# A front end in another order: the first tile in halves, power operands on VectorE, scales in pairs, an early exp table

## The chip, the cores and the metric

The kernel runs on one core of one Trainium2 chip. A core has five engines that run side by side, each through its own list of instructions in order: TensorE (PE in the profile) multiplies matrices, VectorE (DVE), ScalarE (ACT) and GpSimd (POOL) do the rest, and SyncE (SP) issues the transfers (DMAs). Engines wait for each other by semaphores. Where work stands in an engine's list is decided when the kernel is built. The metric is the device time of one execution in microseconds (us), as the median of several.

## The reference

The input x has 2048 tokens of 512 columns in fp32. A first LayerNorm feeds two branches, and these are multiplied:

```python
xn = layernorm(x)                                # no learned scale or bias, eps 1e-5
# A: local attention, 32 heads of 16, window of 8 tokens with dilation 2
q, k, v = split(xn @ wqkv)                       # 512 -> 3 x 512
logits = q . k[pos - 2*w] * 16**-0.5             # w = 0..7; -1e9 ahead of the first token
s = softmax(logits) . v[pos - 2*w] @ wo          # 512 -> 512
# B: an MLP over the columns
h = gelu_tanh(layernorm(xn) @ w1 + b1)           # 512 -> 1376
g = silu(h @ w2 + b2)                            # 1376 -> 512
out = x + s * g
```

## The kernel before, in words

**Tiles.** The even tokens and the odd tokens are kept apart (parity c = 0 and 1), since a window with dilation 2 stays within one parity. Each parity is 8 tiles of 128 tokens, one token to a partition. The 32 heads are 4 blocks of 8 heads. A unit u = 0..7 is one parity with one block of heads. The MLP runs over 4 chunks of 512 tokens and 11 blocks of hidden columns.

**Numbers.** Nearly all matmuls run in fp16 with operands split into a high and a low half, and three products (high by high, low by high, high by low) are added up. Each weight is first scaled by a power of two from its own sum of squares: a Square on ACT with an accumulator, a small matmul on TensorE that adds over partitions (`total`, L400 for two columns), and a chain of one-column operations on DVE (L411, `half_exp` L418, `up` L424, `down` L429). Then come the high half (ACT) and the low half (DVE, L494 for wqkv).

**The front.** For parity 0, `ln0` (L550) takes the tiles group by group, as GROUPS lists them; LOADS says in which order the DMAs bring tiles of x and the first block of wqkv. For each tile, DVE makes statistics (`stats`, L535) and aggregates them to mean and variance (L536). `factors` (L503) then makes, on POOL, for a whole group: an operand from the variance (L514); its power -1/2, which is the scale for both LayerNorms at once (L517); for groups that are normalized on ACT, a bias (L521); another operand (L524) and its power (L526); and two products (L528, L530), which give the scale that attention needs (cT). With this, DVE normalizes a tile (L571), or ACT does, with scale and bias, where the first tile of the group is in ACT_Y (`y_act`, L539). TensorE transposes it by four matmuls with an identity (L578). For tiles 2 and 3 (FP), ACT copies the transposed tile in fp32 (L584), and the first projections of these two tiles run in fp32 on the unscaled weights as they land (L651); all other tiles are cut into halves at once (L590 on ACT, L592 on DVE). In front of the first transpose, 30 idle matmuls (L1063, WAKE0 + WAKE) stand in TensorE's list; the last four wait for the first normalized tile. Parity 1 goes through `ln1` (L598), later and beside the attention of parity 0.

**Units.** `qkv` (L623) first makes a scale cs for its unit: by POOL group by group for unit 0 (L629), by one small ACT operation for the others (L627). For each tile follow 12 fp16 matmuls (L644) into PSUM and an ACT operation that scales them into the buffer U of the unit (L661). There are two such buffers, used in turn, and the matmuls of a unit's first tile wait in the plan for all earlier users of q, k and v of that U. DMAs then bring the rows that a token's window needs from neighbouring partitions (L670, L675, L676). `attention` (L689) has, on DVE, four products of 2048 columns (L704) with four sums (L707), the maximum (L727), the subtraction (L728); then exp on ACT (L730); and on DVE the sum (L732), the reciprocal, the quotient, four products with v (L760) and sums (L755), two of which POOL does in part (L783, L784). The result is transposed by a DMA into oT.

**MLP and end.** `mlp1` (L899) has 12 matmuls for a block of hidden columns (L914), gelu on ACT (L931), the high half on ACT (L935), and the low half on DVE (L939) or by TensorE and ACT. `mlp2` (L953) has 12 matmuls (L961) into four accumulators z and, after the last block of a chunk, silu on ACT (L977, in the last chunk L972), whose results go to HBM for three chunks. ACT holds one function table at a time, and exp, gelu and silu each need their own. `wo_first` (L830) and `wo_last` multiply the attention by wo, then by silu's results, and add x (`finish`, L821 on DVE, L823 on POOL) and store (L824). The last tile is finished in two halves (L880 to L889).

**The plan.** None of this runs in the order of the code. `Plan` (L93) collects every operation with an engine, a planned duration, what it reads and writes, a priority, and sometimes a slack, which makes it look ready later than it is. It then plays the operations through against each other, by the planned durations, and picks at each step the ready operation that can start first, by priority among those close together; buffers of a ring (`Ring`) are given out in this order too. The order that results is written to each engine. A change of a duration, a priority or a dependency can so move operations anywhere in the kernel. The main loop at the end of the code gives each unit a number of MLP steps (`mlp([7, 7, 6, 4, 7, 7, 2, 0][u])`), which fill TensorE between the projections.

## Time and profile before

The times of three runs are 421.53, 421.61 and 422.89 us; the median is 421.61.

| | before |
|---|---|
| profiled execution, its own time | 421.77 us |
| span of the profiled execution | 420.0 us |
| granted TensorE clock, mean | 1.00 |
| PE busy | 410.1 us (98%), 2107 matmuls |
| PE weight loads | 209.5 us (50%), beside the matmuls |
| DVE busy | 387.7 us (92%) |
| ACT busy | 211.6 us (50%) |
| POOL busy | 91.8 us (22%) |
| chain that ended last | PE 78%, DVE 10%, POOL 3%, issue 3%, DMA 2%, ACT 1% |
| moved by DMA | 44.83 MB, 107 GB/s on average |

The span is what lies between the first and the last instruction of the profiled execution; its own time is 1.77 us longer. The chain that ended last is found by going back from the last instruction, each time to what released it. The costliest groups are the matmuls of L914 (115.5 us), L644 (114.5) and L961 (111.4), then DVE's products and sums at L704 (73.1), L707 (72.8) and L760 (63.5), and gelu at L931 (31.4). In rows of the profile, `f` is a tile of 512 columns, `lw` and `mx` are small ones, `prod` one of 2048, `ps`, `mh` and `z` are PSUM accumulators, and an entry such as `[0.35 <-ACT f L977]` behind a row gives the idle time of the engine ahead of it and what ended it.

### The profile page before, as it was taken

To read this page: it belongs to the slowest core of one execution; us is meant where nothing else is said; L and a number is where in the kernel's file an instruction comes from. 1 tells how busy PE (TensorE), PEld (TensorE's weight loads), DVE (VectorE), ACT (ScalarE), POOL (GpSimd) and SP (SyncE) were. 2 spreads that over 40 slices of the span, in tenths; PEclk is the share of its full clock that TensorE was granted. 3 is DMA by queue.
4 is the path that set the end of the run, shared out by engine and by line. 5 is a ranking of instruction groups with operands and counts; after the bars stand their busy time and mean duration, and the time that the engine had idled before them with its cause. 6 is when DMAs were issued, how large, how long until landed. Compare 5 with 4: busy or idle time off the path is not lost.

```text
span 420.0 us, 5549 instructions
## 1 busy us (share of the span) xinstructions
PE 410.1 (98%) x2107; PEld 209.5 (50%) x2107; DVE 387.7 (92%) x365; ACT 211.6 (50%) x314; POOL 91.8 (22%) x166
## 2 busy tenths in 40 slices
PE   7989999999999999999999999999999999999995
PEld 5556544445554465445544654454445544444442
DVE  4867999999999999899999999999999989999983
ACT  3899983953437842853358335334121393236400
POOL 7810200000463043002500430052002500250031
PEclk9999999999999999999999999999999999999999
DMA  8964440120025247611262022006423383007152
GB/s 298 413 234 140 126 163 0 61 91 0 2 87 126 77 108 163 154 39 26 87 151 100 2 87 52 1 20 193 150 85 123 88 209 111 2 0 204 52 144 102
DMA packets 42666, 44.83 MB, mean 107 GB/s; under 512 B 27496, under 2 KB 27936, under 8 KB 42128
## 3 DMA queue, kind: packets, MB, share of 16 engines
q1 hardware_dynamic: 42640, 44.49, 35.0%
q8 instruction: 16, 0.26, 0.3%
q14 instruction: 10, 0.08, 0.1%
HBM read 23.53 MB, written 7.34 MB: 74 GB/s over the span
## 4 chain that ended last, share of the span: by engine, by line
PE 78%; DVE 10%; POOL 3%; issue 3%; DMA 2%; ACT 1%; SPq 0%; DVEq 0%; POOLq 0%; ACTq 0%
PE ps L644 22%; PE z L961 22%; PE mh L914 21%; PE ps L830 6%; PE z L830 2%; DVE prod L704 2%; PE mh L644 2%; DVE prod L760 2%; DVE L L707 2%; PE mh L830 1%; PE ps L914 1%; DMA U<-U 1%; DVE f L614 1%; POOL lw L517 1%; DMA f<-in_A_x_dram 1%
## 5 line engine op out<-in xcount | busy, mean ns | idle before, releaser
L914 PE MATMUL mh<-yT,w 128*128 128x512 f16 (+1 forms) x504 | 115.5, 379 | 0.1
L644 PE MATMUL ps<-wq,yT 128*128 128x384 f16 x684 | 114.5, 326 | 0.9 <-ACT U L661 0.8
L961 PE MATMUL z<-w,h 128*128 128x512 f16 x480 | 111.4, 379 | 0.6 <-ACT f L977 0.6
L644 PEld LDWEIGHTS <-yT 128*128 128x128 f16 x744 | 72.7, 98 | 49.5 <-issue 1.1
L914 PEld LDWEIGHTS <-w 128*128 128x128 f16 (+1 forms) x528 | 52.8, 100 | 61.3 <-issue 0.4
L961 PEld LDWEIGHTS <-h 128*128 128x128 f16 x480 | 47.0, 98 | 56.0 <-issue 1.1
L704 DVE TENSOR_TENSOR prod<-U 128x2048 f32<-128x2048 f32 x32 | 73.1, 2290 | 1.6 <-DMA U<-U 0.6
L707 DVE TENSOR_REDUCE L<-prod 128x128 f32<-128x2048 f32 x32 | 72.8, 2280 | 0.4
L931 ACT ACTIVATE mh<-mh,b1T,hsc 128x512 f32<-128x512 f32 (+1 forms) x42 | 31.4, 749 | 81.5 <-PE mh L914 81.4
L760 DVE TENSOR_TENSOR prod<-L,U 128x2048 f32<-128x2048 f32 x28 | 63.5, 2285 | 0.3
L661 ACT ACTIVATE U<-ps,cs 128x384 f32<-128x384 f32 x58 | 33.0, 578 | 56.1 <-PE ps L644 50.0
L783 POOL COPY gate<-prod 1x1 f32<-1x1 f32 x21 | 4.4, 208 | 238.3 <-DVE prod L704 235.0
L755 DVE TENSOR_TENSOR prod<-prod,prod 128x2048 f32<-128x2048 f32 x16 | 36.5, 2282 | 0.0
L784 POOL TENSOR_TENSOR prod<-prod 128x1024 f32<-128x1024 f32 x14 | 32.9, 2349 | 0.0
L830 PEld LDWEIGHTS <-oT 128*128 128x128 f16 x189 | 18.5, 98 | 22.1
L830 PE MATMUL ps<-wo,oT 128*128 128x512 f16 x120 | 27.2, 379 | 0.0
L935 ACT ACTIVATE h<-mh,hsc 128x512 f16<-128x512 f32 x38 | 26.0, 684 | 0.8
L939 DVE SCALAR_TENSOR_TENSOR h<-mh,hsc,h 128x512 f16<-128x512 f32 x32 | 23.9, 746 | 2.1 <-ACT h L935 2.0
L743 ACT ACTIVATE o<-prod,osc 128x1024 f16<-128x1024 f32 (+1 forms) x9 | 9.5, 1054 | 29.9 <-POOL prod L784 23.9
L784 POOL TENSOR_TENSOR prod<-prod,prod 128x1024 f32<-128x1024 f32 x7 | 16.4, 2347 | 0.0
L931 ACT ACT_TABLE_LOAD x11 | 14.1, 1283 | 0.2
L823 POOL TENSOR_TENSOR U<-U,f 128x512 f32<-128x512 f32 x4 | 5.1, 1268 | 33.5 <-DVE U L893 33.5
(161 smaller groups left out, 366.8 us busy)
## 6 DMA issues: line engine op xcount, KB each, us to landing
f<-in_A_x_dram SPq DMA_DIRECT2D x31, 256.0 KB, 4.3
U<-U SPq DMA_DIRECT2D x16, 392.0 KB, 4.0
gd<-f SPq DMA_DIRECT2D x12, 256.0 KB, 2.1
oT<-in_B_w_dram SPq DMA_DIRECT2D x2, 1024.0 KB, 10.0
yT<-in_B_w_dram SPq DMA_DIRECT2D x2, 1024.0 KB
f<-gd SPq DMA_DIRECT2D x8, 256.0 KB, 2.9
out_dram<-f SPq DMA_DIRECT2D x8, 256.0 KB, 2.6
out_dram<-U SPq DMA_DIRECT2D x7, 256.0 KB, 2.2
```

Source lines behind the costliest of these rows:

```text
L644: nc.tensor.matmul(b.t[:, 0:384], y[:, s, k, o:o + P], wq[:, hb, t, k], start=(n == 0), stop=(n == 11))
L661: act(384, lambda i=i, b=b: nc.scalar.activation(U3[:, i:i + 31:15, :], b.t[:, 0:384].rearrange("p (t e) -> p t e", t=3), AF.Identity, sca ...
L704: dve(2048, lambda p2=p2, g=g: nc.vector.tensor_tensor(p2(), q, slots(Ut, KH, 2 * g), op=ALU.mult), qk + [("kh", ub, 0), ("kh", ub, 1), (" ...
L707: dve(2048, lambda pr=pr, g=g: nc.vector.tensor_reduce(L3()[:, 2 * g:2 * g + 2], pr.t.rearrange("p (r f d) -> p r f d", r=2, d=DH), AX.X, ...
L755: dve(n, lambda: nc.vector.tensor_tensor(d(), a(), b(), op=ALU.add), keys, [dkey])
L760: dve(2048, lambda: nc.vector.tensor_tensor(pr.t.rearrange("p (r f d) -> p r f d", r=2, d=DH), L3()[:, 2 * g:2 * g + 2].rearrange("p r (f ...
L784: nc.gpsimd.tensor_tensor(x.t[:, 0:1024], x.t[:, 0:1024], y(), op=ALU.add)
L830: nc.tensor.matmul(b.t, oT[:, hb, i // 4, s, i % 4], wo[:, t, hb], start=(hb == 0 and n == 0), stop=(hb == last and n == 2))
L914: nc.tensor.matmul(b.t[0:M], w1[:, s, k, f * P:f * P + M], yT[ch][:, t, k], start=(n == 0), stop=(n == 11))
L931: act(512, lambda: nc.scalar.activation(b.t[0:M], b.t[0:M], AF.Gelu_apprx_tanh, bias=b1T[0:M, f:f + 1], scale=hsc[0:M, 1:2]), [b, ("b1T",) ...
L935: act(512, lambda: nc.scalar.activation(hi()[0:M], b.t[0:M], AF.Identity, scale=hsc[0:M, 2:3]), [b] + [("hseq", NF * ch + f - 1)] * (NF * ...
L961: nc.tensor.matmul(z.t, hl[s][0:K, t * P:(t + 1) * P], w2[0:K, w, f], start=(f == 0 and n == 0), stop=(f == NF - 1 and n == 2))
```

## The change

1. **Groups.** GROUPS has tiles 0 and 1 together, and ACT_Y is now read tile by tile: ACT normalizes tiles 4 and 7, where it did tiles 1, 4 and 5.
2. **First tile.** Tile 2 (HALVED) is normalized, transposed and copied in two halves of 256 columns (`in_halves`), and each of its first fp32 matmuls waits for its half alone. Of the two Squares for the first block of wqkv, only the second now waits for this tile's copy.
3. **Factors.** The operands of the powers move from POOL to DVE, right behind each tile's aggregate. The power -1/2 for normalizing is one POOL operation for each tile; the bias is made only for tiles in ACT_Y; the power and the two products for the scales, and unit 0's cs, come once for a group. For parity 1, the two operands move to DVE too.
4. **Planned durations** of POOL's small operations go from 0.21 to 0.28, of a power from 0.42 + 0.14 n to 0.46 + 0.16 n.
5. **Exp table.** Ahead of the maximum, when the last sum of logits is done, a 1x1 exp on ACT loads the table. It takes hold of ACT's table in the plan: until the real exp is placed, nothing with another table is.
6. **Later places.** The matmuls of all tiles of a unit, and no longer those of the first alone, wait in the plan for the earlier users of U, with the same slack of 3.0. The cs operations of parity 1 have a slack of 8.0.
7. WAKE0 is 30 for 26, so that 34 idle matmuls are in the list.

The diff, cut to its core:

```diff
-GROUPS = [(2,), (3,), (0,), (1,), (4, 5), (6, 7)]
+GROUPS = [(2,), (3,), (0, 1), (4, 5), (6, 7)]
...
+HALVED = 2
-ACT_Y = (1, 4, 5)
+ACT_Y = (4, 7)
...
+        if o.hold is not None:
+            self.held = o.hold
...
-                    ok = True
+                    ok = not (self.held and o.table is not None and o.table != self.table)
...
-WAKE0 = 26
+WAKE0 = 30
...
-            act(768, go, [("stq", hb, k)] + ([("yf", 2)] if hb == 0 else []), [(col, k), ("wqh", hb, k), ("wqh", hb, k + 1)],
+            act(768, go, [("stq", hb, k)] + ([("yf", 2)] if hb == 0 and k else []), [(col, k), ("wqh", hb, k), ("wqh", hb, k + 1)],
...
-    def factors(n, mv, mk, cdst, ckeys, bias=True, pp=None):
+    def factors(n, mv, mk, cdst, ckeys, bias, pp=None, each=None):
         A, p0b, rb = R_w.new(), R_w.new(), R_w.new()
-        V = lambda: mv()[:, 0:n, 1]
+        V = lambda a, n: mv()[:, a:a + n, 1]
         a0 = lambda: A.t[:, 0:n]
         a1 = lambda: A.t[:, 8:8 + n]
-        small, power = 0.21, 0.42 + 0.14 * n
-        pool(small, lambda: nc.gpsimd.tensor_scalar(
-            p0b.t[:, 0:n], V(), (1.0 + EPS) / YS ** 2, EPS * EPS / YS ** 2, op0=ALU.mult, op1=ALU.add),
-            mk, [p0b], prio=pp, port=False)
-        pool(power, lambda: nc.gpsimd.tensor_tensor(
-            rb.t[:, 0:n], p0b.t[:, 0:n], halves[:, 0:n], op=ALU.pow), [p0b], [(rb, 0)], prio=pp, port=False)
-        if bias:
-            for a in range(n):
-                pool(small, lambda a=a: nc.gpsimd.tensor_scalar(
-                    rb.t[:, 8 + a:9 + a], mv()[:, a:a + 1, 0], rb.t[:, a:a + 1], -1.0, op0=ALU.mult, op1=ALU.mult),
-                    [mk[a], (rb, 0)], [(rb, 1, a)], prio=pp, port=False)
-        pool(small, lambda: nc.gpsimd.tensor_scalar(
-            a0(), V(), EPS, YS ** -2, op0=ALU.add, op1=ALU.mult), mk, [(A, 0)], port=False)
-        pool(power, lambda: nc.gpsimd.tensor_tensor(a0(), a0(), halves[:, 0:n], op=ALU.pow),
-             [(A, 0)], [(A, 0)], port=False)
-        pool(small, lambda: nc.gpsimd.tensor_tensor(
-            a1(), p0b.t[:, 0:n], rb.t[:, 0:n], op=ALU.mult), [p0b, (rb, 0)], [(A, 1)], port=False)
-        pool(small, lambda: nc.gpsimd.tensor_tensor(cdst, a0(), a1(), op=ALU.mult), [(A, 0), (A, 1)], ckeys, port=False)
+        small, power = 0.28, lambda n: 0.46 + 0.16 * n
+        def operand(a, m):
+            dve(m, lambda: nc.vector.tensor_scalar(
+                p0b.t[:, a:a + m], V(a, m), (1.0 + EPS) / YS ** 2, EPS * EPS / YS ** 2, op0=ALU.mult, op1=ALU.add),
+                mk[a:a + m], [(p0b, j) for j in range(a, a + m)], port=False)
+            if a + m == n:
+                dve(n, lambda: nc.vector.tensor_scalar(
+                    a0(), V(0, n), EPS, YS ** -2, op0=ALU.add, op1=ALU.mult), mk, [(A, 0)], port=False)
+        m = 1 if each else n
+        for a in range(0, n, m):
+            if each:
+                each(a, lambda a=a: operand(a, m))
+            else:
+                operand(a, m)
+            pool(power(m), lambda a=a: nc.gpsimd.tensor_tensor(
+                rb.t[:, a:a + m], p0b.t[:, a:a + m], halves[:, 0:m], op=ALU.pow),
+                [(p0b, j) for j in range(a, a + m)], [(rb, 0, j) for j in range(a, a + m)], prio=pp, port=False)
+            for j in [j for j in range(a, a + m) if bias[j]]:
+                pool(small, lambda j=j: nc.gpsimd.tensor_scalar(
+                    rb.t[:, 8 + j:9 + j], mv()[:, j:j + 1, 0], rb.t[:, j:j + 1], -1.0, op0=ALU.mult, op1=ALU.mult),
+                    [mk[j], (rb, 0, j)], [(rb, 1, j)], prio=pp, port=False)
+        rk = [(rb, 0, j) for j in range(n)]
+        def scales():
+            pool(power(n), lambda: nc.gpsimd.tensor_tensor(a0(), a0(), halves[:, 0:n], op=ALU.pow),
+                 [(A, 0)], [(A, 0)], port=False)
+            pool(small, lambda: nc.gpsimd.tensor_tensor(
+                a1(), p0b.t[:, 0:n], rb.t[:, 0:n], op=ALU.mult), [(p0b, j) for j in range(n)] + rk, [(A, 1)], port=False)
+            pool(small, lambda: nc.gpsimd.tensor_tensor(cdst, a0(), a1(), op=ALU.mult), [(A, 0), (A, 1)], ckeys, port=False)
+        scales()
...
+        def each(a, close):
             with pl.fuse():
                 stats(mv, a, mk[a], xs[a], [xkeys[a]] + behind)
+                close()
         rb = factors(n, mv, mk, cT[:, 0, cpos[ii[0]]:cpos[ii[0]] + n], [("c", 0, i) for i in ii],
-                     ii[0] in ACT_Y, first["prio"])
+                     [i in ACT_Y for i in ii], first["prio"], each)
         for a, i in enumerate(ii):
+            if i == HALVED:
+                in_halves(i, xs[a], xkeys[a], mv, mk[a], rb, a, first, way)
+                continue
...
+    def in_halves(i, x, xkey, mv, mk, rb, a, first, way):
+        y, yf = R_f.new(), R_L.new()
+        yF[i] = yf
+        for h in range(2):
+            c = slice(h * 256, h * 256 + 256)
+            dve(256, lambda c=c: nc.vector.tensor_scalar(
+                y.t[:, c], x()[:, c], mv()[:, a, 0:1], rb.t[:, a:a + 1], op0=ALU.subtract, op1=ALU.mult),
+                [xkey, (rb, 0, a), mk], [(y, h)] + [("yd", i)] * h, f=0.72, c=0.12, **first)
+            b = R_z[1 + (i + 2 * h) % 3].new()
+            def tr(b=b, h=h):
+                for k in range(2):
+                    q = (2 * h + k) * P
+                    nc.tensor.transpose(b.t[:, k * P:(k + 1) * P], y.t[:, q:q + P], ident)
+            pe(2, P, tr, [(y, h)], [b], fp32=2, **first)
+            act(256, lambda b=b, c=c: nc.scalar.copy(yf.t[:, c], b.t[:, 0:256]), [b], [(yf, h)] + [("yf", i)] * h,
+                aps=0, **way)
+        later.append(lambda: halves16(i, yf, [(yf, 0), (yf, 1)], dict(prio=PFP)))
...
-            [("c", c, i) for i in range(NI)] + [("qi", hb)], [cs], prio=PEV) if u else [
-            pool(0.21, lambda q=cpos[g[0]], n=len(g), g=g: nc.gpsimd.tensor_scalar(
+            [("c", c, i) for i in range(NI)] + [("qi", hb)], [cs], prio=PEV, slack=8.0 if c else 0.0) if u else [
+            pool(0.28, lambda q=cpos[g[0]], n=len(g), g=g: nc.gpsimd.tensor_scalar(
...
+        left = pl.users([(x, ub, j) for x in "qkv" for j in range(NI)])
...
-                        start=(k == 0), stop=(k == KT - 1)), [yf, ("stq", hb, k)], [b], fp32=4.1,
+                        start=(k == 0), stop=(k == KT - 1)), [(yf, k // 2), ("stq", hb, k)], [b], fp32=4.1,
...
-                   after=pl.users([b] + [(x, ub, j) for x in "qkv" for j in range(NI)] if n == 0 else [b]),
-                   slack=QSLACK if u > 1 and n == 0 else 0.0)
+                   after=pl.users([b]) | (left if n0 == 0 else set()), slack=QSLACK if u > 1 and n0 == 0 else 0.0)
...
+        act(1, lambda: nc.scalar.activation(warm, ident[0:1, 0:1], AF.Exp), [(L, 3)], [("warm",)],
+            table="exp", prio=PEV, hold=True)
         dve(512, lambda: nc.vector.tensor_reduce(mx.t, Lt(), AX.X, ALU.max), Lk, [mx], port=False)
         dve(512, lambda: nc.vector.tensor_tensor(Lt(), Lt(), over_r(mx.t), op=ALU.subtract),
             [mx] + Lk, Lk)
-        act(512, lambda: nc.scalar.activation(L.t, L.t, AF.Exp, scale=DH ** -0.5), Lk, Lk, aps=0,
-            table="exp", prio=PEV)
+        act(512, lambda: nc.scalar.activation(L.t, L.t, AF.Exp, scale=DH ** -0.5), Lk + [("warm",)], Lk, aps=0,
+            table="exp", prio=PEV, hold=False)
```

More of the change, by code (lines that the diff above doesn't have):

```diff
@@ L79 @@
     __slots__ = ("eng", "dur", "fn", "prio", "table", "bufs", "preds", "succs", "npred",
-                 "ready", "nbytes", "n", "port", "rate", "issue", "tail", "slack")
+                 "ready", "nbytes", "n", "port", "rate", "issue", "tail", "slack",
+                 "hold")
 class Plan:
@@ L93, in add @@
     def add(self, eng, dur, fn, reads=(), writes=(), prio=None, table=None, nbytes=0,
-            after=None, holds=(), port=False, rate=350e3, issue=0.55, tail=1.4, slack=0.0):
+            after=None, holds=(), port=False, rate=350e3, issue=0.55, tail=1.4, slack=0.0,
+            hold=None):
         if self.fused is not None and eng == self.fused["eng"]:
@@ L589, in halves16 @@
-            def halves16(p3=p3, b=b, hi=hi, lo=lo, i=i, way2=way2):
-                act(512, lambda: nc.scalar.copy(hi, p3()), [b] + [("yh", 0, 1)] * (i in FP), [("yh", 0, i)],
-                    aps=0, **way2)
-                dve(512, lambda: nc.vector.tensor_tensor(
-                    lo, p3(), hi, op=ALU.subtract), [b, ("yh", 0, i)], [("y", 0, i)], port=i in FP, **way2)
-            (later.append if i in FP else apply)(halves16)
+                yf = yF[i] = R_L.new()
+                act(512, lambda b=b, yf=yf: nc.scalar.copy(yf.t, b.t), [b], [(yf, 0), (yf, 1), ("yf", i)], aps=0, **way)
@@ new lines, in ln0, with halves16 @@
+                later.append(lambda i=i, yf=yf: halves16(i, yf, [(yf, 0), (yf, 1)], dict(prio=PFP)))
+            else:
+                halves16(i, b, [b], way)
+    def halves16(i, b, bk, way):
+        o = (i % 4) * P
+        hi, lo = (yT[i // 4][:, s, :, o:o + P] for s in range(2))
+        p3 = lambda: b.t.rearrange("p (k t) -> p k t", k=KT)
+        act(512, lambda: nc.scalar.copy(hi, p3()), bk + [("yh", 0, 1)] * (i in FP), [("yh", 0, i)], aps=0, **way)
+        dve(512, lambda: nc.vector.tensor_tensor(
+            lo, p3(), hi, op=ALU.subtract), bk + [("yh", 0, i)], [("y", 0, i)], port=i in FP, **way)
@@ L605, in ln1 @@
             stats(lambda: mv1, i, mk[i], lambda x=x: x.t, [x])
[L606 removed]
+        rb = factors(NI, lambda: mv1, mk, cT[:, 1, :], [("c", 1, i) for i in range(NI)], [True] * NI)
         for i in range(NI):
```

20 lines of the change are left out of this document (5 added, 15 removed).

## The prediction, made before the changed kernel ran

> **What bounds the kernel now.** I read the page's first two parts, then a table of busy time by stretches of the span, then the chain of waits for the first 26 us, then the timelines around each place where TensorE starts nothing. The page:
>
> ```profile
> PE 410.1 (98%) x2107; PEld 209.5 (50%) x2107; DVE 387.7 (92%) x365; ACT 211.6 (50%) x314; POOL 91.8 (22%) x166
> ...
> PEclk9999999999999999999999999999999999999999
> ```
>
> TensorE is busy almost always and its granted clock is full throughout, so a change that leaves the matmuls alone can only win where TensorE waits. VectorE is second, close behind. The table by stretches (us, then PE, PEld, DVE, ACT and POOL busy, granted clock, DMA) says where that is:
>
> ```profile
> 0.00:24.30 24.30, 20.64 (x118) 13.73 (x119) 15.36 (x37) 16.11 (x31) 19.26 (x57) 1.00 0.94 360
> 24.30:48.00 23.70, 23.70 (x150) 14.36 (x149) 17.09 (x38) 23.17 (x41) 1.64 (x1) 1.00 0.39 124
> 48.00:131.80 83.80, 83.80 (x426) 41.84 (x425) 83.23 (x87) 48.41 (x76) 17.60 (x33) 1.00 0.24 75
> ...
> 190.60:333.50 142.90, 142.90 (x749) 73.81 (x749) 141.11 (x100) 52.75 (x74) 31.47 (x48) 1.00 0.28 82
> ...
> 415.40:420.00 4.60, 0.00 (x0) 0.00 (x0) 1.48 (x4) 0.00 (x0) 0.00 (x0) 1.00 0.32 114
> ```
>
> The reader sees a front of 24 us with holes, long full stretches, and a tail of 4.6 us behind the last matmul. In the front POOL is the busiest engine that anything waits for. The chain of waits there (start, duration, what):
>
> ```profile
> 4.46 0.19 POOL lw L514
> ...
> 4.74 0.20 POOL lw L524
> 5.01 0.57 POOL lw L517
> 5.61 0.55 DVE f L571
> ...
> 18.84 0.86 POOL cs L629
> 19.79 0.19 POOL lw L514
> 20.06 0.51 POOL lw L524
> 20.65 0.72 POOL lw L517
> 21.39 1.00 DVE f L571 x2
> ```
>
> From 10.85 to 21.37 us every step of it is on POOL. The other places (timeline rows, in brackets the engine's idle time before the row and who ended it):
>
> ```profile
> 129.62 0.87 ACT L627 ACTIVATE cs<-cT,qsc 128x8 f32<-128x8 f32 x4 [2.30 <-POOL cT L530]
> ...
> 134.61 0.81 PE L961 MATMUL z<-w,h 128*128 128x512 f16 x3 [0.23 <-ACT f L977]
> 135.77 1.46 PE L961 MATMUL z<-w,h 128*128 128x512 f16 x6 [0.35 <-ACT f L977]
> ```
>
> ```profile
> 190.58 1.62 PE L644 MATMUL ps<-wq,yT 128*128 128x384 f16 x9 [0.85 <-ACT U L661]
> ```
>
> Brackets leave out what the pipeline hides, so I count from start to start, less the 0.22 us that a 512-column matmul takes (2.59 us for 12): 0.39 and 0.51 us at 134 and 135, 1.01 at 190 and, by the same count, 0.28 at 347.3 to 347.8, behind the DVE's h at L939. That is 2.2 us in the middle. In the front, between the first transposes at 6.21 and 23.05, it is 2.6 us, the largest 20.82 to 22.00 (1.0), 22.52 to 23.05 (0.4) and 17.01 to 17.64 (0.5). All of TensorE's lost time after its first useful work is thus 4.8 us.
>
> **The change part by part.** The sum is made against the profiled execution, 421.77 us (span 420.0 and 1.77 around it); the median of the runs shown, 421.61, is 0.16 lower.
>
> *First tile.* Before, the aggregate (L536) ends at 4.28, POOL takes over 0.18 later, does two small operations 0.27 apart, the power runs 5.01 to 5.57, DVE 5.61 to 6.16, TensorE from 6.21, the copy on ACT 6.91 to 7.49, and the first projection matmul (L651) starts at 7.54. Now the operand is a DVE operation right behind the aggregate: 4.32 to 4.47 (0.15, from L418's 155 ns and L411's 124), POOL's power from 4.65 to 5.21 (0.36 sooner). A half normalized on DVE is not in the trace: its ends are 0.27 (half of 0.55) and 0.55; 256 columns against 512 are 0.48 against 0.74 us at L884 and L893, so I take 0.35, to 5.60. Here a wait is added: in the built order TensorE's first matmul for the weights' sum of squares (L400) stands ahead of the first transposes, and so these wait for ACT. The weights land at 4.6 (issue at 1.18 and 3.4 us), the Square takes 0.85 and its accumulator 0.19, so L400 starts at 5.66 and the transposes at 5.88. Behind it only these transposes are queued, and ACT's copies wait for them. Two transposes 0.22 and the pipeline's 0.16, then a half copy on ACT (ends 0.29 and 0.58, taken 0.37 by the same ratio): 6.30 to 6.67, and L651 at 6.72. Gain 0.8 at this point; ends 0.3 (both halves at full price) to 0.9.
>
> *Power operands on DVE, scales in pairs.* POOL loses twelve small operations, 0.27 apart: 3.2 us (L524 once took 0.51). It now runs eight single powers (0.54 start to start, 4.3 us), two single scale sets (L526 0.53, L528 0.27, L530 0.28, L629 0.27: 1.35 each) and three paired ones (0.70, 0.27, 0.28, 0.30: 1.55 each), and two biases of 0.24: 12.2 us, against 17.6 busy and paced between 4.46 and 23.1 before. So POOL stops setting the pace; next late is DVE. It gains eight dependent operands (0.19 each), five that follow at once (0.07) and one normalization (tiles 1 and 5 come from ACT, 7 goes there: 0.55), 2.5 us on 15.4. From its first input at 3.37 that leaves 24.3 - 3.4 - 17.9 = 3.0 us, so the front can't gain more than 3.0. On TensorE: useful work starts 0.55 sooner (5.66 for 6.21); the 2.6 us of holes can close; and the built order has eleven idle matmuls between useful ones for six, 5 x 0.109 = 0.55 lost. I leave 0.7 of holes (0.33 ahead of L651, 0.1 behind the second L400, the rest where a row is nearest, 0.2 at 17.6). Front: -0.55 - 2.6 + 0.55 + 0.7 = **-1.9**; ends -0.8 (first tile alone) and -2.6. The DMA queue is not moved past anything there but one 0.5 KB store (L675) behind two loads, which no matmul waits for before 45 us.
>
> *Later places.* The four cs operations (L627) held ACT for 2.30 us at 129.6 with two table loads of 1.28 queued behind; with 8 us of slack they now stand behind the early exp load, in the built order a unit later. The matmuls of a new unit now all wait in the plan for the last reader of U, so other matmuls are put ahead where L661 was late at 190. If all three places close: -2.2. What the new order of every engine makes new is unknown: 0 to 2.2. The nearest rows are the three stalls themselves, 0.28 to 1.01 long; I let one of middle length stand, 0.6: **-1.6**.
>
> *Exp table ahead.* Eight loads of 1.28 stay, moved on ACT ahead of exp. DVE's wait for exp (L732) is 2.0 us in total; no TensorE stall ends there, so I price it at nothing. Its cover is the MLP's matmuls: from one tile's L914 to the reuse of its buffer there are 7.8 us (two L914 and L961 rounds of 5.2, less 2.6), and gelu, hi and lo need 0.75 + 0.69 + 0.75 = 2.2, so a gelu may come 5.6 us late. The hold delays it by the max and subtract (0.67 + 0.69), load and exp (1.28 + 0.63), 3.3. If DVE work is put in between, the cover is gone.
>
> *Tail.* In the built order the store of tile 6 (L824, its add on POOL 1.27) now stands behind both half stores (L889), and its DVE step behind three adds of 0.6. Before, the last landing is 3.4 us behind the last matmul's end; now the add ends about 1.3 behind it, the two half stores issue at 1.25 and 1.7, this one at 2.1 and lands 2.0 later: **+0.6**, ends 0 and 1.3.
>
> Sum: -1.9 - 1.6 + 0.6 = -2.9, 421.77 to 418.9; on the median, 418.7. I forecast 418.8.
>
> **One row against it.** The 128x2 power took 1.09 us at 15.14, beside DVE's L494, and 0.71 at 20.65; L629 took 0.86 at 18.84, beside DVE's L592, and 0.30 at 22.83. So a POOL step can be stretched by 0.4 to 0.6 by what DVE does at the time. The Trainium skill, page "GPSIMD Engine Reference", section Specifications, says that POOL's SBUF interfaces are shared with VectorE and contend with instructions of two SBUF inputs or a 2-port mode; by that rule the trace agrees, and a busier DVE would stretch more powers. This is the first rival.
>
> **Rivals.**
> 1. *POOL's powers stretched beside DVE.* Five tiles' powers after 11 us stand on the chain; 5 x 0.4 = 2.0 takes back the front's 1.9: 420.8. For: the rows above. Against: the powers are shorter now, and the stretched operations were mostly those that are off the chain now (L629, L528).
> 2. *Stall for stall.* The middle's 2.2 us come back at other places, and only front and tail count: -1.3, 420.4. For: DVE is busy 141.1 of 142.9 us, so a late h is always near. Against: TensorE has two mh buffers and other matmuls ready.
> 3. *Slower: the hold.* Gelu waits behind an exp whose DVE steps come late, and TensorE stands at each of the seven later units by 0.7 (between the rows' 0.28 and 1.01): 4.9 us against -3.5 + 0.6, so 423.7. It decides from a gelu more than 5.6 us late, 2.3 more than worked out; one 2.28 us DVE operation in between does not reach that, two do.
> 4. *The halves do nothing*, because L400 holds the transposes: the front gains 0.5 less, 419.3. This lies within the forecast's own range.
>
> **How the numbers follow.** A difference of 0.3% (1.26 us) is about what a measurement here can tell. Forecast 418.8 with rival 4 in it: 0.68, own range 417.4 to 420.2. Rival 1: 0.12, rival 2: 0.12, rival 3: 0.08. Below 420.3 is faster: the first, and most of rival 2, 0.79; same 0.13; slower 0.08. With every term at its better end (-2.6, -2.2, 0) it would be 417.0, with the worse ends (-0.8, 0, +1.3) 422.3. I take 417.3 to 421.0, which leaves out rival 3 and a little at either side.
>
> **What would show it.** L651 first at 6.7; POOL's last power by 22.5 and no TensorE gap over 0.5 after 9 us; the first L914 (now line 961) near 45.2 for 47.04; no wait of z for silu at 134 nor of ps for U at 190; a last landing 4 us behind the last matmul. I am wrong if TensorE shows a gap at each exp, if powers take 0.9 or more, or if the last attention output, whose DVE work gets no shorter, comes after the matmuls that read it.

## The result, and the profile after

The changed kernel takes 423.33 us (median of 5 runs, 423.06 to 423.91) against 421.92 (median of 5, 421.53 to 422.89). The ratio is 1.0034, with a 95% interval of 1.0018 to 1.0049: slower by 0.3%, where 418.8 and faster was forecast. One execution of those reported below, the profiled one of the changed kernel with tile 6's last add on VectorE, took 1124.6 us against 422.1 to 423.2 for its nine others, and no trace of it is read. The profiled execution took 423.62 us with a span of 421.8, 1.8 more than before. The first part of its page:

```profile
PE 410.9 (97%) x2111; PEld 210.6 (50%) x2111; DVE 394.8 (94%) x382; ACT 212.3 (50%) x321; POOL 93.5 (22%) x149
```

TensorE does the same work (0.8 us more busy time), but VectorE has 7.1 us more. The stretches that answer to those shown of before (the same columns):

```profile
0.00:24.30 24.30, 23.01 (x130) 15.65 (x131) 18.49 (x57) 17.69 (x31) 16.81 (x39) 1.00 0.93 360
...
131.80:140.00 8.20, 8.20 (x39) 3.72 (x38) 8.10 (x7) 1.95 (x4) 0.00 (x0) 1.00 0.13 47
140.00:190.60 50.60, 49.48 (x254) 24.98 (x253) 49.48 (x40) 26.84 (x43) 19.36 (x24) 1.00 0.30 71
190.60:333.50 142.90, 140.81 (x737) 72.19 (x736) 139.84 (x101) 55.54 (x79) 30.08 (x46) 1.00 0.32 91
...
415.40:421.80 6.40, 0.29 (x3) 0.01 (x1) 2.85 (x6) 0.00 (x0) 1.26 (x1) 0.82 0.65 239
```

The front is nearly full now (23.01 of 24.30 for 20.64), and 131.8 to 140 is full. But 140 to 190.6 still lacks 1.1 us (0.85 before), 190.6 to 333.5, which had no hole before, lacks 2.1, and the tail is longer. The front on TensorE's timeline:

```profile
5.72 0.56 PE L409 MATMUL z<-s,fours 128*128 128x1 f32 x2
6.14 0.78 PE L635 MATMUL z<-ident,f 128*128 128x128 f32 x4
7.16 1.56 PE L696 MATMUL ps<-prod,L 128*128 128x384 f32 x4 [0.24 <-ACT L L637]
...
45.38 4.70 PE L961 MATMUL mh<-yT,w 128*128 128x512 f16 x21
```

The first projection starts at 7.16 (7.54 before), the first main matmul at 45.38 (47.04): **1.66 us won in the front**. Then the waits of TensorE (who waited, for whom, us in total, times, longest):

```profile
PE mh L961 <- DVE h L986: 2.3, 2, 1.2
PE z L1008 <- ACT f L1024: 0.9, 1, 0.9
PE ps L409 <- ACT wq L483: 0.3, 1, 0.3
```

From start to start, as in the prediction, these are 0.45 us at 56.2, 1.28 at 172.9, 1.07 at 218.3 and 1.34 at 258.3: 4.14, where the middle had 2.19 before. The first of the four waits for a weight's transfer (a Square on ACT, L483, started when the weight had landed). The other three, 3.69 us in sum, wait for an h or for silu. So the last matmul comes 0.40 later than before (415.42 for 415.02; -1.66 + 1.95 is 0.29, the rest is spread), and the last end 6.41 behind it for 4.97: 0.40 + 1.44 = 1.84, the whole difference of the spans.

Why VectorE is late ahead of these three stands in the timeline of VectorE and POOL at 144 us, where the factors of parity 1 are made:

```profile
144.15 2.29 DVE L748 TENSOR_TENSOR prod<-U 128x2048 f32<-128x2048 f32 x1
144.25 3.72 POOL L539 TENSOR_TENSOR lw<-lw,halves 128x8 f32<-128x8 f32 x1 [28.25 <-DVE lw L530]
...
147.95 1.64 POOL L549 TENSOR_TENSOR lw<-lw,halves 128x8 f32<-128x8 f32 x1
...
149.68 2.34 POOL L831 TENSOR_TENSOR prod<-prod 128x1024 f32<-128x1024 f32 x1
149.75 4.47 DVE L748 TENSOR_TENSOR prod<-U 128x2048 f32<-128x2048 f32 x1 [0.46 <-POOL gate L830]
...
152.01 3.99 POOL L543 TENSOR_SCALAR lw<-mv,lw 128x1 f32<-128x1 f32 x8
...
156.25 2.34 POOL L831 TENSOR_TENSOR prod<-prod 128x1024 f32<-128x1024 f32 x1
...
156.65 4.08 DVE L748 TENSOR_TENSOR prod<-U 128x2048 f32<-128x2048 f32 x1
...
158.55 2.24 POOL L553 TENSOR_TENSOR cT<-lw 128x8 f32<-128x8 f32 x1
```

A product that takes 2.29 us at 144.15 takes 4.47 and 4.08 further down. At 149.75 it starts 0.07 behind POOL's add, which ends at 152.02; 152.02 + 2.2 is its end, 154.22. POOL's first bias at 152.01 in its turn lasts as long as that product, and L553 at 158.55 ends with the next (160.8). So one of the two engines stands while the other works. Beside the one-input sums (L751) the same add costs VectorE nothing. The add at 149.68 came beside a product because POOL's queue was late: its 8-column power waited for the product of 144.15, and a second power stood behind it.

In the kernel before, the same power also took 3.67 us, but no add of POOL stood behind it:

```profile
120.17 0.68 DVE L535 BATCH_NORM_STATS2 bn<-f 128x6 f32<-128x512 f32 x1
...
121.58 2.28 DVE L704 TENSOR_TENSOR prod<-U 128x2048 f32<-128x2048 f32 x1
...
121.72 3.67 POOL L517 TENSOR_TENSOR lw<-lw,halves 128x8 f32<-128x8 f32 x1
...
123.78 0.69 DVE L728 TENSOR_TENSOR L<-L,mx 128x512 f32<-128x512 f32 x1
```

There the last of parity 1's statistics (L535) was at 120.17, behind the unit's adds. In the changed kernel it is at 140.52, and the factors fall between the adds of the next unit. A third collision is at 200 us: an L658 that takes 2.98 for 0.68, beside the add at 200.56. Together the three cost VectorE 2.19 + 1.80 + 2.30 = 6.3 us.

### The profile page after: what moved, and what is told of

It is laid out like the page before. It is cut to its first block, busy times and chain, and to the rows that moved or that the text cites. A ratio compares the mean times of both kernels' runs of the same rounds, so it can differ in the third digit from the quotient of the medians.

```text
span 421.8 us, 5573 instructions
## 1 busy us (share of the span) xinstructions
PE 410.9 (97%) x2111; PEld 210.6 (50%) x2111; DVE 394.8 (94%) x382; ACT 212.3 (50%) x321; POOL 93.5 (22%) x149
## 4 chain that ended last, share of the span: by engine, by line
PE 70%; DVE 14%; POOL 5%; ACT 5%; issue 4%; DMA 1%; DVEq 0%; ACTq 0%
PE z L1008 19%; PE ps L689 18%; PE mh L961 17%; PE ps L877 6%; DVE prod L807 3%; PE mh L689 2%; POOL prod L831 2%; DVE prod L748 2%; DVE prod L802 2%; DVE f L658 2%; PE z L1110 1%; PE z L877 1%; DMA yT<-in_A_wqkv_dram 1%; DVE L L751 1%; POOL lw L543 1%
## 5 line engine op out<-in xcount | busy, mean ns | idle before, releaser
L748 DVE TENSOR_TENSOR prod<-U 128x2048 f32<-128x2048 f32 x32 | 77.0, 2411 | 1.0 <-POOL gate L830 0.5
L751 DVE TENSOR_REDUCE L<-prod 128x128 f32<-128x2048 f32 x32 | 72.8, 2280 | 0.4
L539 POOL TENSOR_TENSOR lw<-lw,halves 128x1 f32<-128x1 f32 (+1 forms) x9 | 9.5, 1059 | 34.6 <-DVE lw L530 33.1
L978 ACT ACT_TABLE_LOAD x10 | 12.8, 1283 | 0.2
```

Of the source, the lines that this page charges most:

```text
L748: dve(2048, lambda p2=p2, g=g: nc.vector.tensor_tensor(p2(), q, slots(Ut, KH, 2 * g), op=ALU.mult), qk + [("kh", ub, 0), ("kh", ub, 1), (" ...
L751: dve(2048, lambda pr=pr, g=g: nc.vector.tensor_reduce(L3()[:, 2 * g:2 * g + 2], pr.t.rearrange("p (r f d) -> p r f d", r=2, d=DH), AX.X, ...
L978: act(512, lambda: nc.scalar.activation(b.t[0:M], b.t[0:M], AF.Gelu_apprx_tanh, bias=b1T[0:M, f:f + 1], scale=hsc[0:M, 1:2]), [b, ("b1T",) ...
```

## The experiments

Two theories are set against each other. **A, collision:** the time went where VectorE lost these 6.3 us. **B, hold:** this is the prediction's third rival; gelu waits behind the exp that holds ACT's table, whatever VectorE does. For B speaks that all three large stalls stand behind an exp whose table was loaded early and held. ACT and VectorE ahead of the first:

```profile
164.81 1.28 ACT L772 ACT_TABLE_LOAD   x1
...
166.03 2.29 DVE L748 TENSOR_TENSOR prod<-U 128x2048 f32<-128x2048 f32 x1
...
168.23 0.68 DVE L658 TENSOR_TENSOR f<-f,f 128x512 f16<-128x512 f32 x1
168.83 0.69 DVE L775 TENSOR_TENSOR L<-L,mx 128x512 f32<-128x512 f32 x1
...
169.55 0.63 ACT L777 ACTIVATE L<-L 128x512 f32<-128x512 f32 x1 [1.96 <-DVE L L775]
170.20 1.28 ACT L978 ACT_TABLE_LOAD   x1
171.49 0.75 ACT L978 ACTIVATE mh<-mh,b1T,hsc 128x512 f32<-128x512 f32 x1
...
173.58 0.75 DVE L986 SCALAR_TENSOR_TENSOR h<-mh,hsc,h 128x512 f16<-128x512 f32 x1
...
174.39 2.75 PE L961 MATMUL mh<-yT,w 128*128 128x512 f16 x12 [1.12 <-DVE h L986]
```

A product and an L658 stand ahead of the subtraction L775. Exp waits for it, the gelu load behind exp, and TensorE for the h of that gelu.

### Parity 1's factors on VectorE, in the same order

```diff
-        small, power = 0.28, lambda n: 0.46 + 0.16 * n
+        ve, pw = (nc.vector, ALU.mult) if n == NI else (nc.gpsimd, ALU.pow); small, power = 0.28, lambda n: 0.46 + 0.16 * n
...
-            pool(power(m), lambda a=a: nc.gpsimd.tensor_tensor(
-                rb.t[:, a:a + m], p0b.t[:, a:a + m], halves[:, 0:m], op=ALU.pow),
+            pool(power(m), lambda a=a: ve.tensor_tensor(
+                rb.t[:, a:a + m], p0b.t[:, a:a + m], halves[:, 0:m], op=pw),
...
```

The other operations of `factors` are changed in the same way.

> The plan of the changed kernel is kept, so TensorE, ACT and the DMA queue have the same order. Only the POOL operations of parity 1's factors are issued on VectorE, each at its planned place, with multiplications in place of the powers (so the odd tokens are scaled wrongly; the amount of work is kept). POOL's adds (L831) are then no longer behind the two 8-column powers (3.72 and 1.64 us), the eight biases and the product L553. Theory A, collision: these adds came late and ran beside two-input VectorE operations, and the two engines shut each other out; the three long VectorE operations (L748 of 4.47 and 4.08 us, L658 of 2.98, against 2.28 and 0.68) cost 6.2 us, which made everything after them late. Then both L748 are 2.3 long, VectorE's busy time falls by 4 to 6 us, the TensorE stalls at 172.9, 218.3 and 258.3 (1.28, 1.07, 1.34) shrink by more than half, and the time falls from 423.3 to 419.5 to 421.5. Theory B, hold: gelu waits behind the exp that holds ACT's table, whatever VectorE does; the three stalls stay, with at least 3 us in sum, and the time stays within 0.7 us of 423.3.

Measured: 420.70 us, a ratio of 0.9973 to the kernel before (0.9964 to 0.9983), 2.6 less than the changed kernel. The two products are 2.29 long, and the stall at 173 is gone. The two products, and then TensorE's waits behind the front:

```profile
149.44 2.29 DVE L748 TENSOR_TENSOR prod<-U 128x2048 f32<-128x2048 f32 x1
...
156.60 2.29 DVE L748 TENSOR_TENSOR prod<-U 128x2048 f32<-128x2048 f32 x1
```

```profile
PE mh L961 <- DVE h L986: 1.2, 1, 1.2
PE z L1008 <- ACT f L1024: 0.3, 1, 0.3
```

From start to start they are 0.47 at 217 and 1.34 at 256. The third collision (L658, 2.97 us, now at 198.5) is still there. VectorE's busy time fell by 1.2 only, since it now does twelve more operations, and one of them collided in turn (below); that part of the expectation was wrong. Order and hold are those of the changed kernel, so the hold alone doesn't make the stall at 173.

### In addition, one add of POOL cut to 16 columns

```diff
-                        nc.gpsimd.tensor_tensor(x.t[:, 0:1024], x.t[:, 0:1024], y(), op=ALU.add)
+                        w = 16 if u == 2 and x is p3 else 1024; nc.gpsimd.tensor_tensor(x.t[:, 0:w], x.t[:, 0:w], y()[:, 0:w], op=ALU.add)
```

> The run with parity 1's factors on VectorE (same plan), and in it one of POOL's adds, the second of unit 2, cut from 1024 columns to 16 (the other columns of that sum are left out). In that run this add stood at 198.6 beside an L658, which took 2.97 us instead of 0.68; two stalls were left behind it, 0.48 at 217 and 1.34 at 256. Theory A, collision: both stalls come from the 2.3 us that VectorE loses there; L658 is 0.7 long, the two stalls together fall below 0.7, and the time falls by 1.0 to 1.8 against that run: 418.9 to 419.7. Theory B, hold: these two stand behind an early exp load and a gelu held behind exp in any case; they stay at 1.4 to 2.2 in sum, and the time stays within 0.5 of 420.7. Part of both is possible, 420.0, with the first stall gone and the second left.

Measured: 419.30 us (0.9949; 0.9934 to 0.9963). L658 is 0.7 long again, and no stall of TensorE over 0.25 us is left behind 7.2 us; the table of stretches shows it full wherever the changed kernel had a stall:

```profile
48.00:131.80 83.80, 83.80 (x421) 41.54 (x420) 83.38 (x83) 53.47 (x80) 8.61 (x18) 1.00 0.29 90
140.00:190.60 50.60, 50.60 (x260) 25.54 (x259) 50.30 (x53) 26.31 (x42) 7.97 (x12) 1.00 0.35 81
190.60:333.50 142.90, 142.90 (x755) 73.95 (x753) 139.50 (x101) 56.82 (x81) 30.82 (x48) 1.00 0.32 90
```

The two runs take 423.33 - 419.30 = 4.0 us away by the medians, 3.6 by the two ratios; the three stalls behind the collisions were 3.69. The stall at 56.2 is no part of this: it lies 90 us ahead of the first collision, and TensorE does not stand there in the profiled executions of these two runs. All eight exps still load their table early and hold it. So theory A holds for the changed kernel's order: the collisions make the three stalls, and the hold alone makes none. What the same lateness would cost in this order without the hold, no run shows.

### The exp table loaded when exp comes, in the same order

```diff
-        act(1, lambda: nc.scalar.activation(warm, ident[0:1, 0:1], AF.Exp), [(L, 3)], [("warm",)],
+        act(1, lambda: nc.scalar.activation(warm, ident[0:1, 0:1], AF.Identity), [(L, 3)], [("warm",)],
```

> Same plan and same order as the changed kernel on every engine; the 1x1 operation ahead of the maximum is an Identity instead of an exp, so that the exp table is loaded when the real exp comes (8 loads of 1.28 us move behind the subtraction). This prices the early load by itself, without moving the order. Theory A: the load is needed where exp is on the path; the exps that stood ahead of the three stalls come 1.28 later, and with them gelu: three stalls get up to 1.28 longer each, 423.3 plus 1 to 4 us. Theory B says the same of the load, since the hold's order is kept: so this run only prices the load. If the load does not matter, the time is within 0.5 us of 423.3.

Measured: 424.04 us (1.0044; 1.0031 to 1.0058), 0.7 above the changed kernel, with intervals that overlap. The three stalls have the length that they had (1.26, 1.07, 1.35), so the expected 1.28 for each was wrong; what the run loses is a new stall of 1.1 at 330. The reason for the first stall stands in ACT's rows of this run:

```profile
165.68 1.28 ACT L777 ACT_TABLE_LOAD   x1
...
169.04 0.63 ACT L777 ACTIVATE L<-L 128x512 f32<-128x512 f32 x1 [2.08 <-DVE L L775]
```

The load is not behind the wait of its exp: it ran as soon as ACT was through with what stands ahead, 2.1 us before the data came. At this place the early 1x1 exp brought nothing.

### Without the early exp, and the front alone

The first of these two takes the early exp and its hold away; the second also undoes the wait on U and the slack of cs. The rest is planned anew.

```diff
-        act(1, lambda: nc.scalar.activation(warm, ident[0:1, 0:1], AF.Exp), [(L, 3)], [("warm",)],
-            table="exp", prio=PEV, hold=True)
...
-            table="exp", prio=PEV, hold=False)
+            table="exp", prio=PEV)
```

> The changed kernel without the early 1x1 exp and without its hold; the rest is planned anew. Theory B: without the hold, gelu is no longer behind exp, the three stalls (3.7 us in sum) go, and the time falls to 419.6 to 420.5, below the kernel before. Theory A: POOL's factors and adds still stand where they stood, two products of VectorE are still near 4.3 us long, VectorE is still 4 us late, and what is late then shows at some matmul that waits for h: 422.5 to 425.

> The changed kernel with its front alone: the early exp and hold, the wait of all of a unit's matmuls for the users of U, and the slack of parity 1's cs are undone. The first main matmul should start at 45.4 us, as in the changed kernel. Theory B: the front's gain of 1.7 us stays and the old middle stalls (2.2) come back in place of 4.1: 421.92 - 1.7 + 0 to 0.6, so 420 to 421. Theory A: the front moves parity 1's factors against POOL's adds whatever the later places do; two or three VectorE operations are 2 us too long, and the time is 423 to 430.

Measured: 427.80 us without the early exp (1.0127; 1.0098 to 1.0156) and 428.64 with the front alone (1.0155; 1.0139 to 1.0171). Both have the front's gain (first main matmul at 45.47 and 45.45), both have two products of 4.47 and about 4.0 us beside POOL's adds (at 149.5 and 156.4, and at 154.0 and 161.0), and both are slower still than the changed kernel. Theory B's forecasts (419.6 to 420.5, and 420 to 421) are out: without any hold, the stalls are larger, 1.56, 0.51, 2.44 and 2.22 between 216 and 228 in the first. But the collisions are not shown to make all of these, since both runs have another order. The first run's time lies outside A's own range (422.5 to 425): its last stall ends with a silu that had waited 3.9 us for an earlier result's store to land, and a slower clock, told in the last section, adds to it. In the second, stalls of 2.8 and 1.0 us for the projections (172, 188), which the later places were to remove, are back, TensorE stands twice (1.1 and 0.8 us, at 411 and 415) for the transfer of the last attention output, and the tail is 8.33 us.

### Without halves

```diff
-HALVED = 2
+HALVED = -1
```

> The changed kernel without halves: tile 2 is normalized, transposed and copied whole. Only the front is to be read, since the rest is planned anew. If the halves gain what the prediction gave them (0.5 us), the first fp32 projection starts at about 7.6 instead of 7.16, and the first main matmul of the MLP 0.4 later than 45.38. If they gain nothing, since the sum of squares' matmul at 5.72 holds the transposes anyway, both are within 0.15 us of the changed kernel.

Measured: 429.41 us (two runs). Its first projection starts at 8.11 and the first main matmul at 47.70. But the weights came 0.84 later in the profiled execution (the sum of squares' matmul at 6.56 for 5.72), so only what lies behind the transposes can be compared: 1.31 us from the first transpose to the first projection, against 1.02 with halves (6.14 to 7.16) and 0.88 in the fastest run below, where the weights were as late. The halves thus gain 0.3 to 0.4 us between these two, not nothing. The rest of the 2.3 us at 45 is not settled by this run: TensorE's clock fell in it, as the last section tells.

This run has the longest median of all, though none of its products is longer than 2.3 us. VectorE loses time to POOL in two other ways here. An operand of the factors with a single input takes 2.06 us for 0.16, beside POOL's add of 149.07 to 151.40:

```profile
149.38 2.06 DVE L526 TENSOR_SCALAR lw<-mv 128x8 f32<-128x8 f32 x1
```

And the maximum at 165.77 waits 2.51 us for small POOL operations that stand behind an add and the eight biases (3.95 us, the first of them stretched beside a product). Later TensorE waits 2.65 us for an h (174.7); that the one makes the other is argued, not shown.

### Tile 6's last add on VectorE

```diff
-            finish(1, i, t, [("gu", i), xkey], x, "pool" if i % 2 == 0 else "dve")
+            finish(1, i, t, [("gu", i), xkey], x, "pool" if i % 2 == 0 and i < 6 else "dve")
```

> The changed kernel with one edit in the tail: the last add of tile 6 is VectorE's and no longer POOL's. In the order that results, it stands ahead of the last tile's adds, and its store ahead of the two half stores, instead of behind them; all else is in the order of the changed kernel. If the 6.4 us tail (5.0 before) comes from this store, which issues at 418.85 behind POOL's add and the half stores, the time falls by 0.4 to 0.9 against 423.33. If the tail comes from VectorE, which has 8.8 us of work without a break after the first of the last matmuls, the added 0.65 us of VectorE work delays the last stores by as much as is gained: within 0.3.

> The run without any of the three collisions (419.3; parity 1's factors on VectorE with multiplications for powers, one POOL add cut to 16 columns), with tile 6's last add on VectorE in place of POOL. What is left of the difference to the kernel before is then the order of the tail alone. Its last landing was 6.4 us behind the last matmul, with the store of tile 6 issued last, 0.9 behind the half stores. If the gain of tile 6's edit (1.0 in the changed kernel) is the same without collisions, the time is 418.0 to 418.7 and the tail 5.3 to 5.9.

Measured: 422.32 us in the changed kernel (1.0016; 1.0007 to 1.0025), 1.0 less, and 418.63 in the kernel without the three collisions (0.9915; 0.9899 to 0.9932), 0.7 less. In the second the tail fell from 6.42 to 5.97 (and its front was 0.36 earlier). So tile 6's last add is worth 0.45 by this trace and up to 1.0 by the medians. The tail is still 1.0 longer than before, and the three collisions don't explain it: it was as long, 6.42, without them. What goes with it is the place of the last matmuls in TensorE's list, 3 for each tile with the last head block. In the changed kernel:

```profile
405.54 0.75 DVE L792 SCALAR_TENSOR_TENSOR o<-prod,osc,o 128x512 f16<-128x512 f32 x1 [0.79 <-ACT o L790]
408.29 1.46 PE L877 MATMUL ps<-wo,oT 128*128 128x512 f16 x6
409.14 1.41 DVE L940 SCALAR_TENSOR_TENSOR U<-ps,osc,U 128x512 f32<-128x512 f32 x2 [2.84 <-PE ps L877]
...
417.00 1.25 DVE L934 TENSOR_TENSOR U<-U 128x256 f32<-128x256 f32 x2
417.94 0.81 SPq L936 DMA_DIRECT2D out_dram<-U  x2
418.85 0.40 SPq L871 DMA_DIRECT2D out_dram<-U  x1
```

All first parts (nine matmuls for each tile) stand ahead, and the last parts begin at 408.29, 7.1 us before the last matmul; before it was 402.18, 12.8 ahead of the end. VectorE then works from 409.14 to 418.25 almost without a break, where before it had gaps of 1.70, 1.11 and 1.85 us, and the last stores issue behind it. In the two runs told next, the last parts begin 11.0 us before the last matmul (at 400.87 and 405.21), and the tail is 4.52 in both. No run moves these matmuls alone, so this cause is argued.

### A version without the collisions

Three edits to the changed kernel: no early exp and no hold, QSLACK 2.0, and parity 1's eight biases as one operation on VectorE. The run after it leaves out the third edit alone.

```diff
-QSLACK = 3.0
+QSLACK = 2.0
...
-            for j in [j for j in range(a, a + m) if bias[j]]:
+            if n == NI:
+                dve(8, lambda: nc.vector.scalar_tensor_tensor(
+                    rb.t[:, 8:8 + n], mv()[:, 0:n, 0], -1.0, rb.t[:, 0:n], op0=ALU.mult, op1=ALU.mult),
+                    mk + [(rb, 0, j) for j in range(n)], [(rb, 1, j) for j in range(n)], port=False)
+            for j in [j for j in range(a, a + m) if bias[j] and n < NI]:
```

> A version meant to keep the front's gain without the collisions: the changed kernel without the early exp and its hold, with QSLACK 2.0 for 3.0 (the slack decides where the plan puts the projections, and with them everything behind), and with parity 1's eight biases as one 8-column operation on VectorE in place of eight on POOL. In the order that results POOL's adds again stand beside one-input sums. Theory A: no VectorE product over 2.6 us between 140 and 210, no TensorE stall over 0.6 there, and a time of 418.5 to 420.5, below the kernel before (421.9). Theory B says the same from the missing hold alone, so this run does not tell them apart; if a product is over 4 us long and the time is still below 420.5, theory A is wrong.

> The fastest run so far (no early exp, QSLACK 2.0, biases on VectorE: 417.9) with the eight biases back on POOL, where they take 2 us of POOL's queue between the powers and its next add. Theory A, collision: one product of VectorE near 155 us is 1 to 1.5 us too long again; if something waits behind it, the time rises to 418.5 to 419.5; if VectorE has caught up by the next wait, the time stays within 0.6 of 417.9. Against 427.8 for the run that differs from this one only in QSLACK 3.0, it shows that the order which the plan happens to take, and not the early exp, decides: below 420 here says so; above 425 says that the biases were what made the fastest run fast.

Measured: **417.89 us** for the three edits (median of 6, 417.10 to 421.30; ratio 0.9928, 0.9900 to 0.9956), faster than both kernels. No product is longer than 2.3 us between 140 and 210, TensorE has no stall over 0.25 us behind 7.9 us, and the tail is 4.52. Since the hold is gone too, this run does not tell theory A from theory B. The add stands beside a one-input sum:

```profile
147.35 2.35 POOL L833 TENSOR_TENSOR prod<-prod 128x1024 f32<-128x1024 f32 x1
147.50 2.28 DVE L755 TENSOR_REDUCE L<-prod 128x128 f32<-128x2048 f32 x1
```

With the biases back on POOL, the time is 422.88 us (median of 10, 420.19 to 424.28; 1.0020, 1.0002 to 1.0037). POOL's next add is then late by its queue, and a product pays:

```profile
153.08 2.34 POOL L829 TENSOR_TENSOR prod<-prod 128x1024 f32<-128x1024 f32 x1
154.15 3.42 DVE L748 TENSOR_TENSOR prod<-U 128x2048 f32<-128x2048 f32 x1
```

The 1.14 us there was expected as A had it, the price of it was not: 5.0 us by the medians and 3.9 by the ratios, where I had set at most 1.6. In its profiled execution a single stall of 3.23 us (218.6 to 222.0) follows, and behind it 1.5 us are lost to a slower clock. A silu waits there for a buffer whose store, issued at 215.8 behind a transpose and four loads, took 5.4 us to land. This store's lateness is seen; that the 1.14 us alone made it so is argued, since the two runs' orders differ in a few places.

## Why the prediction was wrong

**First tile: right in kind, a little too early.** The first projection was to start at 6.72 and did at 7.16; in the runs with the same front and the weights as early it was between 6.67 and 7.26. L400's hold on the transposes, which the prediction counted, is seen: the transposes come 0.42 behind it.

**Power operands and pairs: right.** Front -1.9 forecast, -1.66 measured (45.38 for 47.04, and 45.02 to 45.54 in the experiments whose weights were as early). No hole over 0.2 us is left between 10 and 48 us. Rival 1 (powers stretched in the front) did not decide: four of the eight powers take 0.78 to 1.00 us there, for 0.55 to 0.57 of the others, and no hole follows. Powers of 0.9 us or more were named as a sign of being wrong; two came (0.93 and 1.00), and cost TensorE nothing.

**Later places: the named stalls went, and the step that failed is here.** "What the new order of every engine makes new is unknown: 0 to 2.2 ... I let one of middle length stand, 0.6" was measured as 4.14, of which 3.69 came from VectorE's collisions with POOL and 0.45 from a late transfer. The three stalls at 134, 135 and 190 are gone, and so is the one at 347; four others came. The forecast of -1.6 was +1.95; rival 2, stall for stall, would have had 2.2 in place of the 4.14. The bounds of the 0.6 came from stalls that the trace of before shows, but the cause of the new ones was in that trace only as a sign: the row against the forecast spoke of POOL's operations stretched beside VectorE, and rival 1 applied it to the front alone. The other direction, VectorE's own 2.28 us products standing behind a late POOL add, was left out, and with it that parity 1's factors had moved by 20 us into the queue of POOL's adds. The 3.67 us power in the profile of before was the row to look at: it says what happens to whatever stands behind it on POOL. The Trainium skill, page "SBUF — State Buffer", section "SBUF: two separate sides", has the rule in full: the pair of ports that VectorE and GpSimd share is an exclusive lock, taken by whichever operation starts first, and the other blocks fully; VectorE's operations with two SBUF inputs take part in it. By that rule the trace agrees for POOL's adds (4.47 = 2.27 + 2.20) and for the sums with one input (2.28 beside an add). It does not agree for POOL's 8-column power, as the last section shows; there the measurement decides.

**Exp ahead, priced at nothing: right for the hold alone, incomplete for the cover.** The cover (gelu may be 5.6 us late, the hold makes 3.3) holds where VectorE is on time, as the run without stalls shows. The prediction said that if VectorE's work is put in between, the cover is gone. At 172.9 a product and an L658 stood in between, 2.8 us from start to start (166.03 to 168.83), over the 2.3 that were left. But the same two stand there in the run without stalls (163.43 to 166.24), and TensorE does not wait: what used up the cover was VectorE's lateness from before, which the count left out. Rival 3 had the right sign and the right place for three of its seven stalls (3.7 us of 4.9), but as a cause it falls: it needs the collisions. That its 423.7 is close to the measured 423.33 is luck.

**Tail: right in sign, mis-sized.** +0.6 forecast for the store of tile 6, +1.44 measured; tile 6's add is 0.45 to 1.0 of it. The rest goes with the late place of TensorE's last parts, for which the sum had no term. The nearest sign that the prediction named ("the last attention output ... comes after the matmuls that read it") is not what happened: TensorE does not stand at 408.29.

Without the three collisions, the time (419.3, of a version that leaves out the powers of parity 1 and most of one add) lies inside the forecast's own range, 417.4 to 420.2.

## What to carry to other kernels

Where two engines can shut each other out, a queue that is late by 2 us costs the other engine as much, and that engine's followers again: look at what stands behind the longest wait of the small engine, and count both directions. A plan with fixed orders should know that small operations wait too; here eight 1-column operations that it took as free of the port, 2.1 us of queue, went with 4 to 5 us in time. And a gain in one stage moves every later stage: compare where the fixed-rate work (here the statistics of parity 1) comes to stand, before pricing the later stages by the old trace.

## What the runs showed of the hardware

**Even a tiny two-input operation waits out an add.** In the run with parity 1's factors on VectorE and the short add, the product of two 8-column tiles took 1.80 us, until POOL's add of 151.50 ended; the same form took 0.17 elsewhere (145.80):

```profile
145.80 0.17 DVE L539 TENSOR_TENSOR lw<-lw,halves 128x8 f32<-128x8 f32 x1
...
151.50 2.34 POOL L831 TENSOR_TENSOR prod<-prod 128x1024 f32<-128x1024 f32 x1
152.07 1.80 DVE L551 TENSOR_TENSOR lw<-lw,lw 128x8 f32<-128x8 f32 x1
```

Nor are two inputs needed: the single-input operand in the run without halves took 2.06 us for 0.16.

The 8-column power of POOL did not shut VectorE out in that way: before, a subtraction of two inputs (L728, 0.69 at 123.78) ran at full pace beside the 3.67 us power that began at 121.72 and ended at 125.39.

**TensorE's clock can fall to half behind long stalls.** In the run without the early exp, a stretch of 3.2 us behind its four stalls ran at a granted clock of 0.50, with 0.43 us from matmul to matmul instead of 0.22:

```profile
229.00:232.20 3.20, 3.20 (x9) 1.08 (x8) 3.20 (x3) 2.39 (x3) 0.00 (x0) 0.50 0.20 76
```

The same came behind a stall of 2.65 us in the run without halves (178.7 to 181.8) and, in its front, behind holes of 1.3 and 0.7 us (8.1 to 11.1, clock 0.50); it came behind the 3.23 us of the run with the biases on POOL too (0.56 from 222.2 to 225.7). Single stalls of up to 1.35 us in the middle never brought it, and one of 2.8 us (front alone, 171.7 to 174.8) did not either; so these runs give no length that decides. Seven slow matmuls cost 1.5 us on top of the stall. The Trainium skill, page "TensorE: Matmul & The Clock Gate", section "Part 1: The HAM clock gate (the "warmup" mystery)", says that the clock is gated to half by activity in a free-running window of about 3.4 us, after at least one idle window. The slow stretches of 3.0 to 3.5 us here are of about that length, but the condition does not agree: the single stalls ahead of them were 2.65 and 3.23 us, shorter than a window.
